# Gated linear attention and a two-layer MLP: block decay on TensorE and ScalarE, groups of two, a new order of work

## The chip, the cores and the metric

The kernel runs on one core of one Trainium2 chip. The metric is the device time of one execution in microseconds (us). Engines are named TensorE (PE in the profile, its weight loads PEld), the vector engine (DVE), ScalarE (ACT), GpSimd (POOL) and SyncE (SP, which only issues DMAs).

## What is computed

Two stages, the second fed by the first. The first is a gated recurrence over 768 steps for 4 x 8 heads of 48 values; the second is an MLP with a squared ReLU over the 3072 resulting rows of 384 values.

```python
def _attn_ref(q, k, v, alpha):
    state = np.zeros((B, H, D, D))
    for t in range(S):
        state = alpha[:, :, t, :, None] * state + np.einsum('bhd,bhe->bhde', k[:, :, t], v[:, :, t])
        y[:, :, t] = np.einsum('bhd,bhde->bhe', q[:, :, t], state)

def _moe_ref(x, w_in, w_out, s, b):
    h = x @ w_in
    r = np.maximum(h, 0.0)
    return (s * (r * r) + b) @ w_out
```

`w_in` is 384 x 2048, `w_out` 2048 x 384; all inputs and the output are float32, the matmuls run in bf16.

## The kernel before

**Tiling.** The 4 sequences of 768 steps are cut into 24 blocks of 128 steps, 6 to a sequence. Blocks 0 to 3 are done as two pairs (`pair_...`), blocks 4 to 23 one by one (`st_...`). For each block:

- `st_ln` (ScalarE) takes the logarithm of alpha; `st_cum` (TensorE) sums it over time with a triangular matrix, into `cum_ps`, a part of the PSUM bank `ct_ps`.
- `st_exp_b` and `st_exp_i` (ScalarE) give b, the running decay, and its inverse.
- `st_qb` (L433) and `st_kb` (L438), on the vector engine, scale q by b and k by the inverse. `st_vcast` (L427, GpSimd) casts v to bf16.
- `st_Tdma` (L455) transposes scaled q and k with one DMA transpose issued from ScalarE's queue. Blocks 0 to 3 are transposed on TensorE instead.
- `st_A` (L506) forms the scores q k^T, `st_mask` (L515, vector engine) masks them, and `st_y` (L544) forms the output from scores and v, and from q and the state of the block before.
- `st_KV` (L464) forms k^T v in a bank given by `p_of(n)` (`ct_ps` from block NKV on, `py_ps` before). `st_t1` (L485, L489) adds it to the state, and `st_snew` (L500, GpSimd) multiplies the sum by the decay of the whole block, the tile `blast`.
- `st_yevac` (ScalarE) copies the output from PSUM into `xd`, the input of the MLP.

**The block decay.** `blast` holds, for each head and key index, the decay over the block's 128 steps, laid out over partitions. Blocks 0 to 3 get it on TensorE: the logarithms are multiplied with a column of ones, and a small exponential follows. From block NBL = 4 on, `st_bl` gets it from the last row of b: a copy of 32 rows on GpSimd into `b_row` (L417), and two small DMAs from GpSimd's queue that spread the row over partitions (L422). The last block of a sequence needs none. All this is float32.

**The MLP.** The blocks are taken in groups of one or two (`GROUPS`). `mm1` (L709) multiplies weights with a group's `xd` into one of two banks, 512 columns at a time (4 slices of the hidden layer for a group of one, 2 for a group of two). `relu` (L718, ScalarE) and `square` (L724, vector engine) fill a ring of 12 blocks (`gt`), `mm2` (L771) multiplies by `w_out` in four quarters for each block, `oevac` (L782) scales and adds the bias, and `ostore` (L795) writes out: from SP, and for block STQ = 18 from GpSimd's queue. The weights arrive in eight parts, cast by the engines listed in `CE`.

**What sets the order.** There is no automatic scheduling. The class `Schedule` gets every step with its engine, an expected duration, a priority and the tiles it reads and writes; it lays the steps out in expected time, engine by engine, and emits them in that order. The priority is a due time: `want(n)`, from the block's place, `UNIT` and `LEAD`, plus an offset for each kind of step from the table `P`. Each engine runs its instructions in the emitted order and waits where a tile isn't ready. NAY is the block from which scores of block n and the output of block n - 1 are emitted together; NKV is named above. Until the first second-layer matmul, `fill` puts matmuls on zeros into TensorE's expected idle time.

Of the kernel before, what the change touches and what calls it, by code (L numbers as in the profile page):

```python
# [8 lines left out]
FP32 = mybir.dt.float32  # L9
BF16 = mybir.dt.bfloat16  # L10
# [4 lines left out]

VW = 144

GROUPS = [2, 2, 1, 1, 1, 1, 1, 1, 1, 1, 1, 2, 2, 2, 1, 2, 2]
UNIT = 0.295
LEAD = {1: 165.9, 2: 313.7, 4: 51.3}  # L20

NPE = 4

NAY = 10

RING = 12

# [4 lines left out]
TP = 1.45  # L32
LATE = 2.5
NY = 2
NKV = 10
NR2 = 2
STQ = 18
NBL = 4
TBL = 1.7
BLP = 49.5  # L40
TC2 = ["DVE", "DVE"]
VC2 = ["ACT", "ACT"]
CE = ["ACT", "DVE", "ACT", "ACT", "ACT", "ACT", "ACT", "ACT"]
TC = dict(ACT=1.4, DVE=0.87, POOL=2.0)
FILL_GAP = 0.2
COLD = 9.0

P_BM, P_CS, P_BMM = -5, -264.9, 436.0
P = dict(
    ln=60.4, cum=-21.17, eb=-43.71, ei=-25.37, vc=49.76, qb=-0.52, kb=0.09, T=60.15,  # L50
    Tc=-13.57, KV=3.78, t1=-20.78, sn=117.05, Ay=-30.04, A=-44.0, mk=-19.93, y=-36.45,
    ye=18.77, m1=-13.74, re=21.48, sq=1.75, m2=-13.14, oe=-42.62, vm=-2.86, ci=404.27,
    co=-1295.27, ls=140.41, vn=85.16,
)

LOADS = ["V0", "i0", "A0", "K0", "Q0", "A1", "V1", "Q1", "i1", "K1", "i2", "i3", "v4", "o0", "o1", "o2", "o3", "a4", "k4", "q4"]
# [1 line left out]
class Schedule:  # L58
# [8 lines left out]
    def op(self, eng, dur, prio, fn, *args, r=(), w=(), lat=0.08, lock=False):  # L67
        me = len(self.ops)
        deps = set()
        for x in r:  # L70
            if x in self.writer:
                deps.add(self.writer[x])
        for x in w:
            if x in self.writer:
                deps.add(self.writer[x])
            deps.update(self.readers.get(x, ()))
        for x in r:
            self.readers.setdefault(x, []).append(me)
        for x in w:
            self.writer[x] = me  # L80
            self.readers[x] = []
        self.ops.append((eng, dur, prio, fn, args, deps, lat, lock))
# [67 lines left out]
def kernel(  # L150
# [12 lines left out]
    nc = tc.nc  # L163
    ctx.enter_context(tc.manual_schedule())

    B, H, S, D = q.shape
    C = 128
    HC = C // 2
    NCH = S // C
    NP = H // 2  # L170
# [6 lines left out]
    sb = ctx.enter_context(tc.tile_pool(name="sb", bufs=1))  # L177
# [15 lines left out]
    def p_of(n):  # L193
        return (ct_ps if n >= NKV else py_ps)[:, 0:384].rearrange("a (p e) -> a p e", p=NP)

    def many(name, n, shape, dtype, zero=None):
        tiles = []
        for i in range(n):
            t = sb.tile(shape, dtype, name=f"{name}{i}")
            if zero is not None:  # L200
                zero.memset(t, 0.0)
            tiles.append(t)
        return tiles
# [63 lines left out]
    for j in range(2):  # L267
        part = mask2[HC * j : HC * j + HC].rearrange("a (j p) -> a j p", j=2)
        nc.gpsimd.affine_select(
            out=part,  # L270
            in_=part,
# [15 lines left out]
    b_sb = [b_all[:, i] for i in range(2)]  # L287
# [2 lines left out]
    qkT_all = sb.tile([128, 4, 2, NP, 128], BF16, name="qkT")  # L290
    qkT_sb = [qkT_all[:, i] for i in range(4)]
    am_sb = many("am", 2, [128, 2, NP, 128], BF16)
    blast_all = sb.tile([128, 4, NP], FP32, name="blast")
    nc.vector.memset(blast_all, 1.0)
    b_row = sb.tile([128, 2, 2, D, NP], FP32, name="b_row")
    blast_sb = [blast_all[:, i] for i in range(4)]
    xd_sb = many("xd", 3, [128, 3, 512], BF16)
    r_sb = many("r", 2, [128, 512], BF16)
# [91 lines left out]
    def st_cum(n):  # L390
        la = la_sb[n % 2]
        nc.tensor.matmul(  # L392
            out=cum_ps, lhsT=U_bf, rhs=la[:, :, 0:D], start=True, stop=True
        )
        if n % NCH == NCH - 1 or n >= NBL:
            return
        laf = la.rearrange("a h d -> a (h d)")
        for p in range(NP):
            nc.tensor.matmul(
                out=bl_ps[:, p : p + 1],  # L400
                lhsT=laf[:, 128 * p : 128 * p + 128],
                rhs=ones_col_bf,
                start=True,
                stop=True,
            )
# [3 lines left out]

    def st_exp_i(n):  # L410
        nc.scalar.activation(out=binv_sb[n % 2], in_=cum_ps, func=AF.Exp, scale=-1.0)  # L411
        if n % NCH != NCH - 1 and n < NBL:
            nc.scalar.activation(out=blast_sb[n % 4], in_=bl_ps, func=AF.Exp)

    def st_bl(n):
        rows = slice(C - 32, C)
        nc.gpsimd.tensor_copy(  # L417
            out=b_row[rows, n % 2].rearrange("a e d p -> a p e d"),
            in_=b_sb[n % 2][rows].rearrange("a (p e) d -> a p e d", e=2),
        )  # L420
        for e in range(2):
            nc.gpsimd.dma_start(  # L422
                out=blast_all[64 * e : 64 * e + D, n % 4, :], in_=b_row[C - 1 : C, n % 2, e]
            )

    def st_vcast(n):
        nc.gpsimd.tensor_copy(  # L427
# [251 lines left out]
    blk_group = []  # L679
    for g, m in enumerate(GROUPS):  # L680
        blk_group += [(g, t) for t in range(m)]
# [11 lines left out]
    quads = []  # L693
    for g, m in enumerate(GROUPS):
        per = 4 // m
        for u in range(NJ // per):
            units.append((g, [u * per + i for i in range(per)]))
        for tt in range(m):
            for jq in range(NJ // 4):
                quads.append((g, tt, jq))  # L700
    first_blk = [sum(GROUPS[:g]) for g in range(len(GROUPS))]

    def mm1(w):
        g, js = units[w]
        n = GROUPS[g] * C
        hp = h_ps[w % 2]
# [13 lines left out]
    def square(w):  # L720
        g, js = units[w]
        m, s0 = GROUPS[g], first_blk[g] % RING
        r = r_sb[w % 2].rearrange("a (i s t) -> a i s t", i=len(js), s=m)
# [75 lines left out]
    op = sched.op  # L799
    NG = len(GROUPS)  # L800

# [3 lines left out]
    def last(n):  # L805
        return n % NCH == NCH - 1

    def want(n):
        g, t = blk_group[n]
        return (4 * n - LEAD[GROUPS[g]]) * UNIT  # L810

# [21 lines left out]
    for rank, item in enumerate(loads):  # L833
        t, i = rank - 1000, int(item[1:])
# [15 lines left out]
        if st >= NST:  # L850
            reuse.append((len(sched.ops), [(x, h) for x in ("AQ", "KV")[st % 2]]))
        eng = CE[st]
        if item[0] == "i":
            op("SP", TW, t, load_w_in, i, st, w=key, lat=2.0)
            op(eng, TC[eng], P["ci"], cast_w_in, i, st, eng, r=key, w=[("wib", i)], lock=eng != "ACT")
        else:
# [3 lines left out]
               w=["colpart" if i else "colsum"], lock=True)  # L860
# [10 lines left out]
    def pb(n):  # L871
        return "ct" if n >= NKV else "py"

# [6 lines left out]
    def add_block(n):  # L880
        i2, i3, ii, s4 = n % 2, n % 3, n % NIN, n % 4
        t = want(n)
        qT = [("qkT", s4, 0), ("qkT", s4, 1)]
        vp = [("vp", s4, 0), ("vp", s4, 1)]
        if n < N1:
            if n % 2 == 0:
                add_pair(n // 2)
            c = n % 2
            op("PE", 0.5, t + P["KV"], pair_KV, n,
               r=[("kb", s4 - c), ("kb", s4 - c + 1), ("vp", s4, c), ("vc", n // 2 % 2, c)],  # L890
               w=[pb(n)], lat=0.16)
            finish_block(n)
            return
        if n >= N1 + NIN:
            for x in "aqkv":
                load_op(x, n)
        op("ACT", 0.45, t + P["ln"], st_ln, n, r=[("a", ii)], w=[("la", i2)])
        op("PE", 0.27 if n < NBL and not last(n) else 0.16, t + P["cum"], st_cum, n, r=[("la", i2)], w=["ct"], lat=0.16)
        op("ACT", 0.41, t + P["eb"], st_exp_b, n, r=["ct"], w=[("b", i2)])
        if n < NBL and not last(n):  # L900
            op("ACT", 0.49, t + P["ei"], st_exp_i, n, r=["ct"], w=[("bi", i2), ("bl", s4)])
        else:
            op("ACT", 0.41, t + P["ei"], st_exp_i, n, r=["ct"], w=[("bi", i2)])
            if not last(n):
                op("POOL", TBL, t + BLP, st_bl, n, r=[("b", i2)], w=[("bl", s4)], lat=3.4)
        op("POOL", 0.5, t + P["vc"], st_vcast, n, r=[("v", ii)], w=vp, lock=True)
        op("DVE", 0.48, t + P["qb"], st_qb, n, r=[("q", ii), ("b", i2)], w=[("qb", s4)], lock=True)
        op("DVE", 0.48, t + P["kb"], st_kb, n, r=[("k", ii), ("bi", i2)], w=[("kb", s4)], lock=True)
        if n < NPE:
            op("PE", 0.45, t + P["T"], st_T, n, r=[("qb", s4), ("kb", s4)], w=["ct"], lat=0.16)  # L910
            op("DVE", 0.61, t + P["Tc"], st_Tcopy, n, r=["ct"], w=qT)
        else:
            op("ACT", 1.25, t + P["T"], st_Tdma, n, r=[("qb", s4), ("kb", s4)],
               w=[("tq", s4)] + qT, lat=0.1)
            op("SP", 1.95, -3000, lambda: None, r=[("tq", s4)], w=qT, lat=2.0)
        if not last(n):
            op("PE", 0.17, t + P["KV"], st_KV, n, r=[("kb", s4)] + vp, w=[pb(n)], lat=0.16)
        finish_block(n)
# [40 lines left out]
    def finish_block(n):  # L959
# [9 lines left out]
        rA, wA = qT, ["a"]  # L969
        late = n + 1 < NBLK and n + 1 >= NAY  # L970
        if n >= NAY:
            r1, w1 = ys.pop(n - 1)
# [12 lines left out]
    def add_group(g):  # L985
# [7 lines left out]
        for u in range(NJ // per):  # L993
            w = unit_i
            unit_i += 1
            js = units[w][1]
            t = w * UNIT
            op("PE", {1: 0.67, 2: 0.656, 4: 0.648}[m], t + P["m1"], mm1, w,
# [5 lines left out]
        for u in range(4 * m):  # L1004
# [5 lines left out]
            ob = (x // 4) % 2  # L1010
            t = (x + 4 * m + P["m2"]) * UNIT
            op("PE", 0.65, t, mm2, x,
# [18 lines left out]
    for n in range(NBLK):  # L1031
        add_block(n)

        if n and n >= NAY and blk_group[n - 1][0] != blk_group[n][0]:
            add_group(blk_group[n - 1][0])
        if (n + 1 < NAY or n + 1 == NBLK) and n + 1 == first_blk[blk_group[n][0]] + GROUPS[blk_group[n][0]]:
            add_group(blk_group[n][0])
# [46 lines left out]
```

## Time and profile before

| what | value |
|---|---|
| median of 3 runs | 190.92 us (190.63 to 192.15) |
| the profiled execution | 190.63 us, of which its span 188.9 us |
| granted TensorE clock, mean | 0.991 |
| bytes moved by DMA | 35.51 MB, mean 188 GB/s |
| ScalarE: relu (L718), 96 of them | 55.7 us |
| vector engine: square (L724), 96 / mask (L515), 24 | 42.5 / 29.3 us |
| DMA transposes, issue to landing | 2.7 to 7.7 us, median 4.6 |

How to read it: all times are from one execution, counted from the start of its span. A row names a line of the kernel, the engine, the operation, the tile written and those read. Busy time is given with the mean duration of one instruction; behind the bar stands how long the engine sat idle just before such instructions, and what ended most of that. The 40-digit rows cut the span into 40 slices of 4.7 us; a 9 is a share of 90% or more. Matmuls overlap, so a matmul's duration (some 0.22 us for 128 columns) is longer than the distance from one start to the next, and distances between starts tell what TensorE can do. The profile follows the chain of waits only from 94.24 us on.

### The profile page before, as it was taken

Reading aid. Unit: us, or ns where it says so; the run is one execution under the profiler, and the core shown is the slowest. Engines: PE = TensorE matmul, PEld = TensorE weight load, DVE = VectorE, ACT = ScalarE, POOL = GpSimd, SP = SyncE. Lnnn points to the kernel's source line nnn. Section 1 sums busy time; section 2 is a strip of 40 time slices with the busy share of each in tenths; the row PEclk is TensorE's granted clock in tenths of the full one; section 3 lists DMA queues with packets and bytes.
Section 4 is the critical chain, followed back from the end, with each engine's and each line's share of the span. In section 5 each row is a group of like instructions: output and inputs, shape, how many; then the busy total and the mean of one; then the engine's idle time right before and its main releaser. Section 6 shows DMA issues by size and latency. Waiting matters only on the chain. (4 is left out here: it accounts for less than half of the span.)

```text
span 188.9 us, 5578 instructions
## 1 busy us (share of the span) xinstructions
PE 172.8 (91%) x2232; PEld 124.0 (66%) x2232; DVE 139.6 (74%) x252; ACT 106.3 (56%) x200; POOL 71.1 (38%) x118
## 2 busy tenths in 40 slices
PE   6669987899999997999999999999969999999992
PEld 2245765566776875877776767777647786778672
DVE  2468999998688788967877797979756987464421
ACT  3466899943553863655564555856515753566400
POOL 7973022255506356323645553334436532010000
PEclk9999999999999999999999999999979999999999
DMA  5999998999999999998998999999697693011012
GB/s 157 358 341 372 347 372 220 210 159 247 219 183 211 243 125 229 181 219 183 211 208 169 182 188 230 187 210 210 131 164 168 112 213 96 9 42 45 33 51 83
DMA packets 120985, 35.51 MB, mean 188 GB/s; under 512 B 114256, under 2 KB 119376, under 8 KB 120960
## 3 DMA queue, kind: packets, MB, share of 16 engines
q1 hardware_dynamic: 98688, 29.70, 67.5%
q10 hardware_dynamic: 21120, 5.25, 20.0%
q0 software_dynamic: 1152, 0.22, 0.7%
q8 instruction: 17, 0.28, 0.6%
q14 instruction: 8, 0.07, 0.1%
HBM read 25.17 MB, written 4.72 MB: 158 GB/s over the span
## 5 line engine op out<-in xcount | busy, mean ns | idle before, releaser
L718 ACT ACTIVATE r<-h_ps 128x512 bf16<-128x512 f32 x96 | 55.7, 599 | 38.1 <-PE h_ps L709 14.9
L709 PE MATMUL h_ps<-xd,w_in_bf 128*128 128x128 bf16 (+1 forms) x816 | 74.6, 243 | 0.7 <-ACT r L718 0.7
L771 PE MATMUL o_ps<-w_out_bf,gt 128*128 128x384 bf16 x368 | 71.0, 328 | 1.4 <-ACT w_out_bf L324 1.3
L709 PEld LDWEIGHTS <-w_in_bf 128*128 128x128 bf16 x816 | 61.3, 98 | 11.8 <-issue 2.2
L724 DVE TENSOR_TENSOR gt<-r 128x512 bf16<-128x512 bf16 x96 | 42.5, 457 | 15.3 <-ACT r L718 14.5
L771 PEld LDWEIGHTS <-gt 128*128 128x128 bf16 x368 | 34.3, 98 | 19.5 <-issue 1.9
L417 POOL COPY b_row<-b_s 32x384 f32<-32x384 f32 x16 | 17.2, 1077 | 42.4 <-ACT b_s L408 40.0
L515 DVE TENSOR_TENSOR am<-a_ps,mask 128x1024 bf16<-128x1024 f32 x24 | 29.3, 1220 | 3.7 <-PE a_ps L506 3.5
L500 POOL TENSOR_TENSOR s_st<-s_st,blast 128x384 bf16<-128x384 bf16 x16 | 14.2, 887 | 23.5 <-DMA blast<-b_row 10.1
L782 DVE SCALAR_TENSOR_TENSOR o_sb<-o_ps,s_col,bias_w 128x384 f32<-128x384 f32 x23 | 14.1, 615 | 8.2 <-PE o_ps L771 7.9
L422 POOL DMA_DIRECT2D blast<-b_row x32 | 16.7, 526 | 4.7 <-POOL b_row L417 4.7
L689 ACT ACTIVATE xd<-py_ps 128x384 bf16<-128x384 f32 x22 | 11.1, 503 | 10.9 <-PE py_ps L544 3.4
L438 DVE TENSOR_TENSOR qk<-k_in,binv 128x384 bf16<-128x384 f32 x20 | 15.8, 792 | 0.0
L427 POOL CAST vp<-v_in 128x384 bf16<-128x384 f32 x20 | 10.5, 527 | 13.9 <-PE a_ps L506 7.0
L386 ACT ACTIVATE la<-a_in 128x384 bf16<-128x384 f32 x20 | 10.5, 525 | 8.1 <-DVE am L515 2.7
L433 DVE TENSOR_TENSOR qk<-q_in,b_s 128x384 bf16<-128x384 f32 x20 | 12.8, 639 | 2.6 <-ACT b_s L408 2.4
L408 ACT ACTIVATE b_s<-ct_ps 128x384 f32<-128x384 f32 x20 | 9.8, 492 | 4.9 <-DVE gt L724 2.6
L506 PE MATMUL a_ps<-qkT 64*128 64x128 bf16 x192 | 9.6, 218 | 1.7 <-DMA qkT<-qk 1.3
L506 PEld LDWEIGHTS <-qkT 64*128 64x128 bf16 x192 | 5.5, 94 | 7.9 <-issue 4.7
L411 ACT ACTIVATE binv<-ct_ps 128x384 f32<-128x384 f32 x20 | 9.9, 493 | 0.0
L489 DVE TENSOR_TENSOR s_st<-ct_ps,s_st 64x192 bf16<-64x192 f32 x18 | 6.4, 354 | 4.0 <-PE ct_ps L464 2.0
L544 PE MATMUL py_ps<-am,vp 128*32 128x128 bf16 x352 | 8.8, 219 | 0.0
(92 smaller groups left out, 128.9 us busy)
## 6 DMA issues: line engine op xcount, KB each, us to landing
out_dram<-o_sb SPq DMA_DIRECT2D x22, 192.0 KB, 2.7
v_in<-in_v_dram SPq DMA_DIRECT2D x20, 192.0 KB, 4.5
a_in<-in_alpha_dram SPq DMA_DIRECT2D x20, 192.0 KB, 4.3
k_in<-in_k_dram SPq DMA_DIRECT2D x20, 192.0 KB, 4.1
q_in<-in_q_dram SPq DMA_DIRECT2D x20, 192.0 KB, 4.6
wst<-in_moe_w_in_dram SPq DMA_DIRECT2D x4, 768.0 KB, 6.8
gt<-in_moe_w_out_dram SPq DMA_DIRECT2D x4, 768.0 KB, 9.6
gt<-in_alpha_dram SPq DMA_DIRECT2D x2, 384.0 KB, 4.5
```

Source lines behind the costliest of these rows:

```text
L417: nc.gpsimd.tensor_copy(out=b_row[rows, n % 2].rearrange("a e d p -> a p e d"), in_=b_sb[n % 2][rows].rearrange("a (p e) d -> a p e d", e=2),)
L422: nc.gpsimd.dma_start(out=blast_all[64 * e : 64 * e + D, n % 4, :], in_=b_row[C - 1 : C, n % 2, e])
L433: nc.vector.tensor_tensor(out=qk_sb[n % 4][:, 0, :, 0:D], in0=q_in[n % NIN], in1=b_sb[n % 2], op=ALU.mult)
L438: nc.vector.tensor_tensor(out=qk_sb[n % 4][:, 1, :, 0:D], in0=k_in[n % NIN], in1=binv_sb[n % 2], op=ALU.mult,)
L500: nc.gpsimd.tensor_tensor(out=s_sb[n % 3], in0=t1_sb[n % 2], in1=bl, op=ALU.mult)
L506: nc.tensor.matmul(out=a_ps[:, e, p, :], lhsT=qkT[64 * e : 64 * e + 64, 1, p, :], rhs=qkT[64 * e : 64 * e + 64, 0, p, :], start=True, stop ...
L515: nc.vector.tensor_tensor(out=am_sb[n % 2].rearrange("a e p t -> a (e p) t"), in0=a_ps.rearrange("a e p t -> a (e p) t"), in1=(mask2 if n ...
L709: nc.tensor.matmul(out=hp[:, i * n : (i + 1) * n], lhsT=w_in_bf[:, kk, 128 * j : 128 * (j + 1)], rhs=xd_sb[g % 3][:, kk, 0:n], start=(kk = ...
L718: nc.scalar.activation(out=r_sb[w % 2], in_=h_ps[w % 2], func=AF.Relu)
L724: nc.vector.tensor_tensor(out=gt_sb[:, s0 : s0 + m, js[0] : js[0] + len(js)].rearrange("a s j t -> a j s t"), in0=r, in1=r, op=ALU.mult,)
L771: nc.tensor.matmul(out=op[:, 0:d_model], lhsT=gt_sb[:, s0, j], rhs=w_out_bf[:, j, :], start=(j == 0), stop=(j == NJ - 1),)
L782: nc.vector.scalar_tensor_tensor(out=ots, in0=o_ps[(x // 4) % 2][:, 0:d_model], scalar=s_col, in1=bias_w, op0=ALU.mult, op1=ALU.add,)
```

## The change

The block decay of blocks 4 to 22 is formed as in blocks 0 to 3: four one-column matmuls on TensorE behind the cumulative sum, and a small exponential on ScalarE behind `st_exp_i`. `st_bl`, `b_row` and its DMAs go, `blast` becomes bf16, and the clearing of `blast` goes. Four blocks form groups of one, where there were ten. The first part of `w_in` is cast by GpSimd instead of ScalarE. k^T v moves to the bank `ct_ps` from block 7 on (block 10 before), scores and output are paired from block 12 (10 before), and all due times are others. Transposes and the output store from GpSimd are the same in both.

```diff
-GROUPS = [2, 2, 1, 1, 1, 1, 1, 1, 1, 1, 1, 2, 2, 2, 1, 2, 2]
-UNIT = 0.295
-LEAD = {1: 165.9, 2: 313.7, 4: 51.3}
+GROUPS = [2, 2, 1, 1, 1, 1, 2, 2, 2, 2, 2, 2, 2, 2]
+UNIT = 0.392
+LEAD = {1: 204.6, 2: 323.1, 4: 100.0}
...
-NAY = 10
+NAY = 12
...
-NKV = 10
+NKV = 7
...
-NBL = 4
-TBL = 1.7
-BLP = 49.5
...
-CE = ["ACT", "DVE", "ACT", "ACT", "ACT", "ACT", "ACT", "ACT"]
+CE = ["POOL", "DVE", "ACT", "ACT", "ACT", "ACT", "ACT", "ACT"]
...
-P_BM, P_CS, P_BMM = -5, -264.9, 436.0
+P_BM, P_CS, P_BMM = -5, -286.4, 473.5
 P = dict(
-    ln=60.4, cum=-21.17, eb=-43.71, ei=-25.37, vc=49.76, qb=-0.52, kb=0.09, T=60.15,
+    ln=34.88, cum=-15.29, eb=-32.24, ei=9.49, vc=73.43, qb=-9.65, kb=14.71, T=95.62,
...
-    blast_all = sb.tile([128, 4, NP], FP32, name="blast")
-    nc.vector.memset(blast_all, 1.0)
-    b_row = sb.tile([128, 2, 2, D, NP], FP32, name="b_row")
+    blast_all = sb.tile([128, 4, NP], BF16, name="blast")
...
-        if n % NCH == NCH - 1 or n >= NBL:
+        if n % NCH == NCH - 1:
             return
         laf = la.rearrange("a h d -> a (h d)")
         for p in range(NP):
...
         nc.scalar.activation(out=binv_sb[n % 2], in_=cum_ps, func=AF.Exp, scale=-1.0)
-        if n % NCH != NCH - 1 and n < NBL:
+        if n % NCH != NCH - 1:
             nc.scalar.activation(out=blast_sb[n % 4], in_=bl_ps, func=AF.Exp)
-
-    def st_bl(n):
-        rows = slice(C - 32, C)
-        nc.gpsimd.tensor_copy(
-            out=b_row[rows, n % 2].rearrange("a e d p -> a p e d"),
-            in_=b_sb[n % 2][rows].rearrange("a (p e) d -> a p e d", e=2),
-        )
-        for e in range(2):
-            nc.gpsimd.dma_start(
-                out=blast_all[64 * e : 64 * e + D, n % 4, :], in_=b_row[C - 1 : C, n % 2, e]
-            )
...
-        if n < NBL and not last(n):
-            op("ACT", 0.49, t + P["ei"], st_exp_i, n, r=["ct"], w=[("bi", i2), ("bl", s4)])
-        else:
-            op("ACT", 0.41, t + P["ei"], st_exp_i, n, r=["ct"], w=[("bi", i2)])
-            if not last(n):
-                op("POOL", TBL, t + BLP, st_bl, n, r=[("b", i2)], w=[("bl", s4)], lat=3.4)
+        op("ACT", 0.49, t + P["ei"], st_exp_i, n, r=["ct"], w=[("bi", i2), ("bl", s4)])
```

The rest of the table `P` is replaced in the same way, and the planner's time for the cumulative sum is that with the four matmuls for all blocks.

More of the change, by code (lines that the diff above doesn't have):

```diff
@@ L46 @@
 COLD = 9.0
-P_BM, P_CS, P_BMM = -5, -264.9, 436.0
+P_BM, P_CS, P_BMM = -5, -286.4, 473.5
 P = dict(
-    ln=60.4, cum=-21.17, eb=-43.71, ei=-25.37, vc=49.76, qb=-0.52, kb=0.09, T=60.15,
-    Tc=-13.57, KV=3.78, t1=-20.78, sn=117.05, Ay=-30.04, A=-44.0, mk=-19.93, y=-36.45,
-    ye=18.77, m1=-13.74, re=21.48, sq=1.75, m2=-13.14, oe=-42.62, vm=-2.86, ci=404.27,
-    co=-1295.27, ls=140.41, vn=85.16,
+    ln=34.88, cum=-15.29, eb=-32.24, ei=9.49, vc=73.43, qb=-9.65, kb=14.71, T=95.62,
+    Tc=-13.62, KV=-13.54, t1=9.55, sn=124.73, Ay=-11.39, A=-22.53, mk=-58.68, y=-13.83,
+    ye=5.65, m1=-19.67, re=9.86, sq=-33.02, m2=-18.25, oe=-24.3, vm=-57.17, ci=324.52,
+    co=-825.8, ls=148.33, vn=-450.01,
 )
@@ L897, in add_block @@
         op("ACT", 0.45, t + P["ln"], st_ln, n, r=[("a", ii)], w=[("la", i2)])
-        op("PE", 0.27 if n < NBL and not last(n) else 0.16, t + P["cum"], st_cum, n, r=[("la", i2)], w=["ct"], lat=0.16)
+        op("PE", 0.27, t + P["cum"], st_cum, n, r=[("la", i2)], w=["ct"], lat=0.16)
         op("ACT", 0.41, t + P["eb"], st_exp_b, n, r=["ct"], w=[("b", i2)])
-        if n < NBL and not last(n):
-            op("ACT", 0.49, t + P["ei"], st_exp_i, n, r=["ct"], w=[("bi", i2), ("bl", s4)])
-        else:
-            op("ACT", 0.41, t + P["ei"], st_exp_i, n, r=["ct"], w=[("bi", i2)])
-            if not last(n):
-                op("POOL", TBL, t + BLP, st_bl, n, r=[("b", i2)], w=[("bl", s4)], lat=3.4)
+        op("ACT", 0.49, t + P["ei"], st_exp_i, n, r=["ct"], w=[("bi", i2), ("bl", s4)])
         op("POOL", 0.5, t + P["vc"], st_vcast, n, r=[("v", ii)], w=vp, lock=True)
```

## The prediction

> **What bounds the kernel now.** I read the page's shares and 40 slices first, then the waits by total, then TensorE's own timeline at the places where it stands still.
>
> ```profile
> PE 172.8 (91%) x2232; PEld 124.0 (66%) x2232; DVE 139.6 (74%) x252; ACT 106.3 (56%) x200; POOL 71.1 (38%) x118
> PE   6669987899999997999999999999969999999992
> PEclk9999999999999999999999999999979999999999
> DMA  5999998999999999998998999999697693011012
> L417 POOL COPY b_row<-b_s 32x384 f32<-32x384 f32 x16 | 17.2, 1077 | 42.4 <-ACT b_s L408 40.0
> L422 POOL DMA_DIRECT2D blast<-b_row x32 | 16.7, 526 | 4.7 <-POOL b_row L417 4.7
> ```
>
> TensorE's row is full from slice 10 to the end save for one dip, in which its clock row falls to 7: after the first 40 us TensorE sets the time, and what can be won is its standing still there. GpSimd is 38% busy, and 33.9 us of its 71.1 are the two decay rows (L417, L422). TensorE's timeline shows the dip:
>
> ```profile
> 136.68 0.41 PE L544 MATMUL py_ps<-am,vp 128*32 128x128 bf16 x16
> 138.83 0.46 PE L464 MATMUL ct_ps<-vp,qk 128*128 128x96 bf16 x4 [1.75 <-POOL vp L427]
> 139.09 1.48 PE L771 MATMUL o_ps<-w_out_bf,gt 128*128 128x384 bf16 x4
> 140.37 2.42 PE L709 MATMUL h_ps<-xd,w_in_bf 128*128 128x256 bf16 x12
> ```
>
> The k^T v product waits 1.75 us for GpSimd's cast of v. The next four second-layer matmuls then take 1.28 us to the next start, against 0.65 us elsewhere, and twelve first-layer ones 2.26 us against 1.31. The chain of waits shows what GpSimd did:
>
> ```profile
> 134.26 0.55 DVE qk L438
> ...
> 134.91 0.93 POOL s_st L500
> 135.84 0.05 issue
> 135.89 1.00 POOL b_row L417
> 136.89 0.28 issue
> 137.17 1.06 POOL blast L422 x2
> 138.23 0.05 issue
> 138.28 0.51 POOL vp L427
> ```
>
> k's scaled tile was ready at 134.81; the cast came 3.5 us later, behind one state product, one copy and two DMA issues. Vector engine rows show a second cost: at 97.17 the same k product (L438) took 1.08 us and at 134.26, with no GpSimd copy beside it, 0.55.
>
> [...]eight of the 20 L438 rows and three of the L433 rows begin while an L417 copy runs and take 0.82 to 1.09 us instead of 0.55, some 5 us in all.[...] eight 2-column matmuls of L585 start at 6.05 and the next matmul at 6.25, 25 ns each.[...] 1.75 us of idleness were followed by 3.5 us at about half rate[...].
>
> **The change, part by part.** The sum is made against the profiled execution, 190.63 us (span 188.9 and 1.73 around it); the median of the runs is 190.92, 0.3 above.
>
> *Decay back on TensorE.* Sixteen blocks (4 to 22 without the last of each sequence) get four one-column matmuls: 64 x 25 ns = **+1.6 us**, on the path since TensorE has no room. ScalarE gets 16 small exponentials; the nearest row (L602, eight columns) lasts 183 ns, so at most 2.9 us, beside a ScalarE that is 56% busy. They stand after both large exponentials, so q's and k's products don't wait for them; a relu behind one does, by up to 0.18 us. I take 0 here and put that into new waits.
>
> *Decay off GpSimd.* 16 copies and 32 DMA issues go. Four stalls of TensorE go with them: 1.75 (above), 0.17 at 94.28 (also for the cast), 0.25 at 98.31 (for the k product stretched to 1.08 us), and 0.37 at 101.01 (the cumulative sum waits for the state sum, L489, which waits for the state product at 99.37, behind a copy and two issues): **-2.5 us**. The half-rate stretch costs 0.63 + 0.95 + 0.09 = 1.7 us. It begins with the stall, so I take **-1.7**; a 1.34 us wait at 72 us has none after it, so its bounds are 0 and -1.7. The small DMAs are 0.7% of DMA time: 0. The decay as bf16 changes no row that TensorE waits for now: 0.
>
> *Groups.* Six blocks go from groups of one to groups of two. A one-block group's 24 narrow matmuls take 1.35 us per half (48.74 to 50.09), so 2.68 a block; twelve wide ones take 1.31 us, 2.62 a block. 6 x 0.06 = **-0.4 us**. TensorE issues one filler matmul fewer, some **-0.2** before the first second-layer matmul.
>
> *First weight cast on GpSimd.* ScalarE did it in 1.47 us at 11.66. GpSimd's cast row is 527 ns for 384 columns; four times that is an estimate of 2.1 us, from 11.5 to 13.6. Behind it on GpSimd's queue are the second pair's four casts of v (from 12.54 to 13.6) and the state product at 15.51, which slips by some 0.5 us. Their readers are the shift on TensorE at 15.40 and the output of block 2 after 25: hidden. The first reader of the weights starts at 17.84. ScalarE's logarithm of pair 1 moves up, but the sums behind it hold their place on TensorE after block 1's output, so no gain. I take 0, bounds -0.5 and +0.5[...].
>
> *New order.* I counted TensorE's work between producer and consumer in both instruction orders with the rates above. From a block's cumulative sum to its score product (the way through both exponentials, the products and the DMA transpose) the 20 blocks have 7.6 to 11.6 us now, eight of them at most 8.5; in the new order 7.8 to 13.3, four at most 8.5. The one stall there now (1.34 us at 73.39, for a transpose) belongs to block 8, which goes from 8.0 to 9.0: I take half, **-0.7**, bounds 0 and -1.3. Other distances shrink. From cumulative sum to k^T v, three blocks (12, 16, 20) fall to 2.9 us and four (8, 9, 13, 21) to 3.4 to 3.6; the work takes 1.8 us when nothing is in the way (133.00 to 134.81) and 2.0 to 3.3 in other places. From scores to output, blocks 4, 7, 8 and 9 have 1.9 to 2.2; the trace needs 1.9 (44.60 to 46.49). From k^T v to the next sum, blocks 8 and 9 have 1.2, since k^T v now moves to the shared bank (ct_ps) at block 7 instead of 10; the trace needs 1.2 when the vector engine is free (106.06 to 107.24). Nine or so of these at 0.2 us each: **+1.8**, bounds 0 and +6, for nothing in the trace before shows them. The store of block 18 stays on GpSimd, last in its queue, now with no decay ahead: 0. On SP the stores stand a few places earlier or later among the loads; SP's loads mostly wait for buffers, and the load that came last ahead of a cast (3.4 us late at 156.27) stopped only GpSimd. At the end 52 instead of 36 second-layer matmuls follow the last first-layer one: same work, no gap now, 0.
>
> *Sum:* +1.6 - 2.5 - 1.7 - 0.4 - 0.2 - 0.7 + 1.8 = -2.1. From 190.63 that is 188.5; from the median 188.8. I say **188.6 us**, 1.2% faster. The case's own range, with the clock stretch kept or no new waits, is 187.0 to 190.0.
>
> **Rivals.** (a) *The gain is eaten by the order.* New waits come to 3.5 to 4.5 us, or loads and transposes, with the DMA row at 9 in nearly every slice to 150 us, push back when TensorE runs ahead. For it: the distances above, and landing times of the transpose from 2.7 to 7.7 us. Against: some 0.5 us a block goes from the way to the transpose, and fewer blocks are near the limit. Time: 188.5 + 2.2 = 190.7. (b) *A stall of the shared bank, slower.* At blocks 8 and 9 the cumulative sum waits for the state sum. If that stands behind a score mask (1.22 us) on the vector engine, the sum, both exponentials and the transpose come 1.2 us later, and scores in turn. Two places where that grows to the size of the stall at 138.83, each followed by a half-rate stretch, cost 2 x (1.75 + 1.7) = 6.9 us in place of the 1.8: 193.6. It decides once new waits pass 6.1 us (192.8). Against: vector load falls by the 5 us of stretched products. (c) *The decay was no burden.* GpSimd's stalls come back at the cast for another reason (a late load of v, 6.3 us of waits in three places now); only +1.6 - 0.6 and the new waits count: 191.6 without these, 193.4 with 1.8 of them. The instruction order shows the copies and issues gone, so the change does do what it says.
>
> **How the numbers follow.** Forecast 0.50, (a) 0.20, (b) 0.18, (c) 0.12. About 1%, 1.9 us, is what can be told from no change, so faster means under 189.0. Of the forecast 0.40 lies below that and 0.10 above; a little of (a) lies below: faster 0.43. Same: 0.10 + 0.16 + 0.06 = 0.32. Slower: (b), half of (c) and an edge of (a): 0.25. The range, 186.9 to 193.4, leaves out a tenth on each side: below, no new waits with the startup bound; above, most of (b).
>
> **What would show it.** Right: no L417 or L422 rows; GpSimd near 39 us busy; L438 near 0.55 us mean (0.79 now) outside state products; TensorE's waits on the cast under 0.3 us; no clock below 9 after 20 us; 64 one-column matmuls adding 1.6 us. Wrong: TensorE waiting over 4 us after 40 us for DVE (s_st, am, qk) or qkT, a first second-layer matmul later than 28.5 us, or a new half-rate stretch.

## The result and the profile after

| | before | after |
|---|---|---|
| median of 4 runs each, same chip | 190.85 us (190.63 to 192.15) | 185.22 us (184.53 to 185.95) |
| ratio, 95% interval | | 0.9692 (0.9634 to 0.9749) |
| profiled execution, span | 190.63, 188.9 us | 185.07, 183.4 us |
| granted TensorE clock, mean | 0.991 | 1.000 |

The changed kernel is 5.6 us faster; 2.1 to 2.3 were forecast, and the time lies below the range. Measured again beside other experiments it had a ratio of 0.9812 (0.9764 to 0.986) and 186.63 us, so "some 2 to 3%" is what can be said of its gain; the two intervals do not overlap. The direction was right; the size was too small, by a factor of 2.5 in the first pair and of about 1.7 in the second.

The page after, the shares and slices that answer to those of before, and two rows of its groups:

```profile
PE 171.9 (94%) x2151; PEld 122.8 (67%) x2151; DVE 135.4 (74%) x251; ACT 106.0 (58%) x215; POOL 39.6 (22%) x71
PE   6678987999999999999989999999999999999993
PEclk9999999999999999999999999999999999999999
DMA  5999999999999999899999999999965992000112
L411 POOL CAST vp<-v_in 128x384 bf16<-128x384 f32 x20 | 11.9, 593 | 63.8 <-DMA v_in<-in_v_dram 63.8
L422 DVE TENSOR_TENSOR qk<-k_in,binv 128x384 bf16<-128x384 f32 x20 | 11.6, 582 | 1.1 <-DMA k_in<-in_k_dram 1.0
```

The dip of TensorE's row and of its clock is gone, GpSimd is busy 39.6 us instead of 71.1, and no row of a copy or a DMA issue of the decay is left. k's product (L422 now, L438 before) has fallen from a mean of 792 ns to 582. DMA is as full as before (194 GB/s in the mean, 188 before), so the gain does not come from there.

The table splits each span at the start of the first second-layer matmul (`mm2`) and at the end of the last matmul, and gives the sum of TensorE's waits after 40 us.

| part, us | before | after | difference |
|---|---|---|---|
| up to the first second-layer matmul | 28.15 | 27.22 | -0.93 |
| from there to the last matmul's end | 157.21 | 153.05 | -4.16 |
| after it | 3.56 | 3.09 | -0.47 |
| within the middle: TensorE's waits after 40 us | 4.60 (7 places) | 1.81 (5 places) | -2.79 |
| within the middle: half-rate stretch | 1.7 | none | -1.7 |
| within the middle: wait for the column sums | 0.89 | 0.26 | -0.63 |

With +1.6 for the one-column matmuls, -0.4 for wider groups and +0.2 for a wait on the second weights' cast, the last three rows make -3.7 of the -4.2. TensorE's waits before, by what it waited for, those that matter here (total us, times, longest):

```profile
PE ct_ps L464 <- POOL vp L427: 1.9, 2, 1.8
...
PE a_ps L506 <- DMA qkT<-qk: 1.3, 1, 1.3
...
PE o_ps L373 <- DVE colsum L356: 0.9, 1, 0.9
PE h_ps L709 <- ACT r L718: 0.7, 2, 0.4
```

and after:

```profile
PE h_ps L693 <- ACT r L702: 0.8, 2, 0.5
...
PE py_ps L528 <- DVE am L499: 0.3, 1, 0.3
PE o_ps L755 <- DVE gt L708: 0.3, 1, 0.3
PE ct_ps L448 <- POOL vp L411: 0.3, 1, 0.3
PE o_ps L368 <- DVE colsum L351: 0.3, 1, 0.3
```

Nothing that TensorE waits for after 40 us in this trace is late by more than 0.5 us. The wait for the cast has shrunk to 0.30 us in one place, and the transpose isn't waited for at all. (In a second trace of the changed kernel three waits are left, of 0.72, 0.54 and 1.07 us: a relu, a transpose and that same cast. Ahead of the cast GpSimd stands idle in both traces, for v's load.) The third line of before is one that the prediction passed over. Its cause stands in the timeline of before, all engines, at the place where the column sums for the bias are folded:

```profile
36.53 1.11 POOL L417 COPY b_row<-b_s 32x384 f32<-32x384 f32 x1 [6.38 <-ACT b_s L408]
36.82 1.06 DVE L356 TENSOR_TENSOR colsum<-colsum 128x384 f32<-128x384 f32 x1
```

The fold starts while a GpSimd copy of the decay runs and takes 1.06 us, and TensorE waits for it. After, the groups with different shapes kept apart show:

```profile
L351 DVE TENSOR_TENSOR colsum<-colsum 128x384 f32<-128x384 f32 x1 | 0.6, 551 | 0.0
...
L394 PE MATMUL ct_ps<-ones_col_bf,la 128*128 128x1 bf16 x64 | 3.9, 164 | 0.0
```

Half the time, without the copy. The second row is the price of the change: the 64 one-column matmuls. Its "busy" 3.9 us is not their cost, since matmuls overlap; four of them take 0.10 us from the first's start to the next matmul's (60.54 to 60.64), 1.6 us in all.

### The profile page after: what moved, and what is told of

It is laid out like the page before. It is cut to its first block, busy times and chain, and to the rows that moved or that the text cites. A ratio compares the mean times of both kernels' runs of the same rounds, so it can differ in the third digit from the quotient of the medians.

```text
span 183.4 us, 5347 instructions
## 1 busy us (share of the span) xinstructions
PE 171.9 (94%) x2151; PEld 122.8 (67%) x2151; DVE 135.4 (74%) x251; ACT 106.0 (58%) x215; POOL 39.6 (22%) x71
## 4 chain that ended last, share of the span: by engine, by line
PE 44%; DVE 3%; DMA 2%; issue 1%; ACT 1%; ACTq 1%; SPq 0%; POOL 0%; POOLq 0%
PE o_ps L755 19%; PE h_ps L693 17%; PE py_ps L528 3%; DMA v_in<-in_v_dram 2%; PE a_ps L490 2%; PE o_ps L724 1%; PE ct_ps L448 1%; DVE gt L708 1%; PE ct_ps L387 1%; ACT r L702 1%; DVE o_sb L766 1%; ACTq L439 1%; DVE qk L422 1%; DVE am L499 0%; PE h_ps L724 0%
## 5 line engine op out<-in xcount | busy, mean ns | idle before, releaser
L693 PE MATMUL h_ps<-xd,w_in_bf 128*128 128x256 bf16 (+1 forms) x672 | 73.2, 257 | 0.9 <-ACT r L702 0.8
L702 ACT ACTIVATE r<-h_ps 128x512 bf16<-128x512 f32 x96 | 55.1, 600 | 28.4 <-PE h_ps L693 9.4
L755 PE MATMUL o_ps<-w_out_bf,gt 128*128 128x384 bf16 x368 | 69.1, 326 | 1.9 <-ACT w_out_bf L319 1.5
L693 PEld LDWEIGHTS <-w_in_bf 128*128 128x128 bf16 x672 | 56.2, 98 | 10.7 <-issue 1.5
L411 POOL CAST vp<-v_in 128x384 bf16<-128x384 f32 x20 | 11.9, 593 | 63.8 <-DMA v_in<-in_v_dram 63.8
L473 DVE TENSOR_TENSOR s_st<-ct_ps,s_st 64x192 bf16<-64x192 f32 x24 | 8.5, 354 | 6.1 <-PE ct_ps L448 5.3
L422 DVE TENSOR_TENSOR qk<-k_in,binv 128x384 bf16<-128x384 f32 x20 | 11.6, 582 | 1.1 <-DMA k_in<-in_k_dram 1.0
L1028 PE MATMUL o_ps<-zeros 128*128 128x512 bf16 x21 | 7.0, 463 | 1.3 <-DVE zeros L236 1.3
L528 PEld LDWEIGHTS <-vp 128*32 128x32 bf16 x384 | 6.5, 97 | 1.2 <-issue 0.7
```

Of the source, the lines that this page charges most:

```text
L411: nc.gpsimd.tensor_copy(out=vp_sb[n % 4].rearrange("a p (x d) -> a p x d", d=D)[:, :, 0:3:2, :], in_=v_in[n % NIN].rearrange("a (p e) d -> ...
L422: nc.vector.tensor_tensor(out=qk_sb[n % 4][:, 1, :, 0:D], in0=k_in[n % NIN], in1=binv_sb[n % 2], op=ALU.mult,)
L528: nc.tensor.matmul(out=y_of(n)[32 * (x % 4) : 32 * (x % 4) + 32, x // 4, :], lhsT=(st[:, p, c0 : c0 + 32] if e is None else vp[:, p, c0 + ...
L693: nc.tensor.matmul(out=hp[:, i * n : (i + 1) * n], lhsT=w_in_bf[:, kk, 128 * j : 128 * (j + 1)], rhs=xd_sb[g % 3][:, kk, 0:n], start=(kk = ...
L702: nc.scalar.activation(out=r_sb[w % 2], in_=h_ps[w % 2], func=AF.Relu)
L755: nc.tensor.matmul(out=op[:, 0:d_model], lhsT=gt_sb[:, s0, j], rhs=w_out_bf[:, j, :], start=(j == 0), stop=(j == NJ - 1),)
```

## The experiments

The question was which part brings the gain: the decay off GpSimd, or the new order with its groups and cast; and within the decay, which of its costs. The kernels of the first four share a chip and a before of 190.21 us (15 runs), the next four one of 190.01 us (12 runs), the last four one of 191.06 us (11 runs).

**1. The decay alone, every engine in the old order.** In the kernel before:

```diff
-        if n % NCH == NCH - 1 or n >= NBL:
+        if n % NCH == NCH - 1:
             return
...
-        if n % NCH != NCH - 1 and n < NBL:
+        if n % NCH != NCH - 1:
...
-                op("POOL", TBL, t + BLP, st_bl, n, r=[("b", i2)], w=[("bl", s4)], lat=3.4)
+                op("POOL", TBL, t + BLP, lambda n: None, n, r=[("b", i2)], w=[("bl", s4)], lat=3.4)
```

> The order of before on every engine, only the decay of blocks 4 to 22 moved from GpSimd and its DMAs to TensorE and ScalarE. Decay theory (GpSimd's copies and DMA issues made TensorE wait, at the cast of v, the state and the stretched vector products): the 1.6 us of one-column matmuls is paid, stalls of 1.75 + 0.17 + 0.25 + 0.37, the half-rate stretch of 1.7, the 1.34 us wait for block 8's transpose and 0.5 us at the fold of column sums go: about 186.5 to 187.5 us. Order theory (the gain is in the new order and the groups of two, the decay itself is neutral): 190.9 + 1.6, 191.5 to 192.5 us.

Measured: 185.7 us, ratio 0.9741 (0.966 to 0.9821). TensorE's waits after 40 us come to 1.29 us in four places, none of them one of the seven of before. The longest, in its timeline:

```profile
140.95 0.40 PE L506 MATMUL a_ps<-qkT 64*128 64x128 bf16 x8 [0.51 <-DMA qkT<-qk]
```

That is a late block. The scores that waited 1.34 us for their transpose at 73.39 before start at 72.83 without a wait. (They are the tenth scores in TensorE's timeline and belong to the sixth of the 20 transposes, so to block 9; the prediction and the expectation call it block 8.) So the decay alone is about the whole gain, and rival (c), that the decay was no burden, falls.

**2. The new order alone, the decay left on GpSimd.** In the changed kernel, `st_bl` as it was before, called directly behind `st_exp_i`'s first exponential for blocks 4 to 22:

```diff
-        if n % NCH == NCH - 1:
+        if n % NCH == NCH - 1 or n >= 4:
             return
...
-        if n % NCH != NCH - 1:
-            nc.scalar.activation(out=blast_sb[n % 4], in_=bl_ps, func=AF.Exp)
+        if n % NCH != NCH - 1 and n >= 4:
+            st_bl(n)
```

> The changed kernel with its new order on every engine, but the decay of blocks 4 to 22 formed by GpSimd's copy and two DMAs, put on GpSimd's queue where the small exponential stood. Decay theory: 1.6 us of matmuls go and 4 to 6 us of stalls come back, 187.5 to 189.5 us. Order theory: 183.6 to 185.5 us.

Measured: 201.82 us, ratio 1.059 (1.0505 to 1.0675). TensorE waited 8.2 us in six places for the cast of v and 3.6 in two for the state sum. What GpSimd did ahead of one such wait, in its timeline:

```profile
59.82 1.06 POOL L419 DMA_DIRECT2D blast<-b_row  x2 [0.29 <-POOL b_row L414]
...
64.81 0.86 POOL L497 TENSOR_TENSOR s_st<-s_st,blast 128x384 bf16<-128x384 bf16 x1 [3.39 <-DMA blast<-b_row]
65.73 0.95 POOL L414 COPY b_row<-b_s 32x384 f32<-32x384 f32 x1
66.98 1.05 POOL L419 DMA_DIRECT2D blast<-b_row  x2 [0.29 <-POOL b_row L414]
68.08 0.50 POOL L424 CAST vp<-v_in 128x384 bf16<-128x384 f32 x1
```

The state product stands 3.39 us for the small DMAs' data (18.1 us in seven places over the kernel), and the cast behind it comes when product, copy and two issues are through. This is the cost of the decay at this place in this order; another place for it, tuned to the order, wasn't tried. Two stretches at half rate after 20 us add to it in this trace (experiment 7). It shows that the order is not a gain by itself, and how much hangs on what is queued ahead of the cast.

**3. The bias product later, in the kernel before.** At 13.48 us, in the startup, TensorE stood 1.47 us for the first state sum on the vector engine. That sum stood behind the product that fills `bones` with the bias, which waited 1.28 us for a small DMA. So the product was moved behind block 1's mask:

```diff
+        if n == 1:
+            bias_mul()
...
-    op("DVE", 0.3, P_BM, bias_mul, r=["b"], w=["bones"], lock=True)
+    op("DVE", 0.3, P_BM, lambda: None, r=["b"], w=["bones"], lock=True)
```

> Before, with one vector instruction (the product of ones with the bias column, which waits for a small DMA) moved from ahead of the first state product to behind the second score mask, where the changed kernel has it. Startup theory (the vector engine's 1.28 us wait there delayed TensorE's first products, and all that follows, by 1 us): 189.7 to 190.1 us. Rival (the delay is absorbed before the first second-layer matmul, which waits for the casts of its weights): 190.7 to 191.0 us.

Measured over 12 runs: 189.83 us, ratio 0.9984 (0.9944 to 1.0025). The wait itself shrank from 1.47 to 0.39 us, and the time didn't move by what can be measured: the first second-layer matmul started at 28.74 us, no earlier than the 28.15 of before. With the old decay still in, the old stalls are there again at nearly the same times, as TensorE's timeline shows:

```profile
72.68 0.40 PE L506 MATMUL a_ps<-qkT 64*128 64x128 bf16 x8 [0.61 <-DMA qkT<-qk]
...
138.51 0.33 PE L464 MATMUL ct_ps<-vp,qk 128*128 128x96 bf16 x4 [1.40 <-POOL vp L427]
```

Block 9's transpose is late by 0.61 us here and the cast at 138 by 1.40; before it was 1.34 and 1.75. They belong to the old decay, not to one execution.

**4. Experiments 1 and 3 together.**

> Both edits in the order of before. If both theories hold and add up: 185.5 to 186.5 us, so that order, groups and the cast on GpSimd are left with less than 1.3 us of the gain. If the new order is needed for more than that: above 187 us.

Measured: 185.18 us, ratio 0.9735 (0.9656 to 0.9813); again beside the changed kernel 186.44 us, 0.9794 (0.974 to 0.9847):

> The order of before with the decay on TensorE and the late bias product, again. From the first second-layer matmul to the last matmul its trace had 151.8 us, the changed kernel's 153.1. If that holds for the time: 0.3 to 0.8% faster than the changed kernel on this chip. If the first 28 us, which differ from run to run, decide: no difference.

The changed kernel once more, on that chip:

> The changed kernel once more, on the same chip and beside the same runs of before as the next two, to put a figure on what the new order, the groups and the cast add to the decay. If they add nothing: within 0.5% of the next run. If they are worth the 1.1 us between the ratios so far: 0.5 to 0.8% below it. Expected ratio to before 0.965 to 0.975.

It gave 186.63 us, 0.9812 (0.9764 to 0.986). On one chip the changed kernel and the old order with the new decay differ by 0.1%, within both intervals. So new order, groups and first cast together add nothing that can be measured. The middle part, from the first second-layer matmul to the last matmul, is 153.1 us in both traces of the changed kernel, 153.3 in experiment 1, 151.8 and 152.1 here.

**5. The parts of the old decay, one by one.** All in the changed kernel, with `blast` still formed by TensorE, so that nobody waits for their results. Only the 16 copies:

```diff
+            if n >= 4:
+                st_bl(n)
+
+    def st_bl(n):
+        rows = slice(C - 32, C)
+        nc.gpsimd.tensor_copy(
+            out=b_row[rows, n % 2].rearrange("a e d p -> a p e d"),
+            in_=b_sb[n % 2][rows].rearrange("a (p e) d -> a p e d", e=2),
+        )
```

> The changed kernel with GpSimd's 16 copies of b's last rows added back, read by nobody: no DMAs, the decay still from TensorE. [...]at least half of the way back from e2, 189 us or more, with the k product near 0.8 us mean. Queue theory (what hurt is GpSimd's time ahead of the cast of v, and the wait of the state product for the small DMAs): 1.1 us a block hides in a GpSimd that is 22% busy; 185 to 187 us.

Measured over nine runs: 188.73 us, ratio 0.9906 (0.9853 to 0.996). "189 us or more" stood for the case that the loss comes from the vector engine's products taking longer beside the copies (k's 792 ns on average before, 582 after). The groups with shapes apart:

```profile
L352 DVE TENSOR_TENSOR colsum<-colsum 128x384 f32<-128x384 f32 x1 | 1.1, 1055 | 0.0
...
L432 DVE TENSOR_TENSOR qk<-k_in,binv 128x384 bf16<-128x384 f32 x20 | 15.7, 785 | 0.5 <-DMA k_in<-in_k_dram 0.5
```

The copies alone bring back both stretched rows, k's product at 785 ns (792 before the change) and the fold at 1055. The fold goes with these copies in all 14 traces: 1.05 to 1.06 us in the five with them (before, experiments 2, 3, this one and copies with issues), 0.55 us in the nine without. TensorE's wait for it is 0.87 to 0.89 us in the five and 0.38 or less in eight of the nine; in the ninth (experiment 6, first kernel) it is 1.16, for a fold that started late and took 0.55.

Only the 32 issues, of a constant row into a tile that nobody reads:

```diff
+    def st_bl(n):
+        for e in range(2):
+            nc.gpsimd.dma_start(
+                out=scr[64 * e : 64 * e + D, n % 4, :], in_=b_row[C - 1 : C, n % 2, e]
+            )
```

> The changed kernel with only the 32 small DMA issues on GpSimd's queue added back, from a constant tile to a tile that nobody reads. They wait for nothing and no engine waits for them. Queue theory in its weaker form (the issuing time of 1.06 us a block is the cost): 187 us or more. If the cost is in waiting for the data: 185 to 186 us.

Measured: 186.69 us, ratio 0.9826 (0.9769 to 0.9884), a little above the changed kernel's 0.9692 and 0.9812 and inside the interval of the second: at most a small cost, and none that these runs can show.

Copies and issues, the issues into the same unread tile:

> Both added back, copies and issues in the places of the run with the decay on GpSimd, but nothing waits for their data, since the decay comes from TensorE. Against that run (201.8 us) it lacks only the wait of the state product and of the first state for the small DMAs, and has the 1.6 us of matmuls. If waiting for the data made most of the loss: under 192 us. If GpSimd's own time made it: 198 us or more.

Measured: 191.69 us, ratio 1.0103 (1.0034 to 1.0172). TensorE waits 5.5 us in seven places for the cast. The parts don't simply add: against the two ratios of the changed kernel, copies alone cost 0.9 to 2.1 points, issues alone 0.1 to 1.3, both together 2.9 to 4.1. The waits suggest why: TensorE waits for the cast once with copies alone (1.23 us) and once with issues alone (1.13), at the one cast that is late in the changed kernel too, and seven times with both. That fits a cast that is late only when what stands ahead of it is longer than its slack. From here to experiment 2 are 10.1 us more (201.82), and what that one adds is the state product's wait for the DMAs' data, against 1.6 us of one-column matmuls that it doesn't have. In its profiled run the two half-rate stretches after 20 us account for some 3 us, an estimate from the spacing of starts in them. The two befores, 190.21 and 190.01, differ by 0.1%.

**6. More casts to GpSimd.** The second part of `w_out` in the changed kernel, to relieve ScalarE (`eng = "POOL" if i == 1 else eng` in `cast_w_out`):

> A try for a faster version: the changed kernel in its order, with the second part of the output weights cast by GpSimd, idle at that time, instead of ScalarE. TensorE waits 0.96 us for that cast now, and ScalarE is free 1.4 us sooner. If the casts set the pace there: 183.7 to 184.7 us. If the column sums on the vector engine set it (TensorE then waits for them before the bias product)[...]: 185 to 186 us.

Measured: 187.7 us, ratio 0.9866 (0.9806 to 0.9926), not faster. TensorE waits 0.8 us for that cast and 1.2 for the fold of the column sums, where the changed kernel's two traces have 0.85 to 0.96 and 0.26 to 0.37: the wait moved.

The first part of `w_in`, as in the change, but in the kernel of experiment 4 with its order kept:

```diff
+        eng = "POOL" if i == 0 else eng
```

> The same order, with the first part of w_in cast by GpSimd instead of ScalarE, the step for which the prediction took 0 with bounds of 0.5 us. Hidden: within 0.5 us of the run without it. If GpSimd's later casts of v for the second pair hold TensorE up: 0.5 to 1 us slower. If ScalarE was late there: 0.5 us faster.

Measured: 184.80 us (184.29 to 185.72), ratio 0.9721 (0.9664 to 0.9777). All six runs lie below all six of the changed kernel on the same chip (186.33 to 186.99), 1.0% in the medians, so this is the fastest version here; the two intervals against before overlap, and so do the ranges of this kernel and of the one without the cast (185.15 to 187.01). It has one stall of TensorE after 40 us, 0.29 us. In the changed kernel's trace this cast took 1.46 us (at 11.58), not the 2.1 that I estimated. Against the same kernel without it, the medians differ by 1.6 us on this chip, but on the chip of the first four that kernel had nearly the same ratio (0.9735). So whether the cast brings anything there is not settled. In the traces TensorE's wait for a weight cast at 20 us went from 0.90 to 0.50 us (for another producer) and one of 0.69 at 52 us is absent, which would be a part of it.

**7. Does a long gap bring the half rate?** The kernel of experiment 4, with three useless GpSimd copies ahead of five casts, to make gaps of different lengths:

```diff
+        if n in (9, 13, 15, 19, 21):
+            for _ in range(3):
+                nc.gpsimd.tensor_copy(out=scr, in_=qk_sb[n % 4])
```

> The same kernel as the second, with three useless copies on GpSimd, which wait for the scaled k of the block, ahead of the cast of v in blocks 9, 13, 15, 19 and 21, so that TensorE waits for that cast as it did at 138.83 before. If every wait of 1.5 us or more starts a half-rate stretch of some 3.4 us: each gap is followed by first-layer matmuls at twice their spacing and costs 1.7 us more than itself. If it is chance: some gaps of 1.5 to 2.8 us are followed by full rate.

One run, 193.28 us, with waits on the cast of up to 1.91 us. TensorE's timeline after the longest:

```profile
97.50 0.33 PE L468 MATMUL ct_ps<-vp,qk 128*128 128x96 bf16 x4 [1.91 <-POOL vp L431]
97.67 1.46 PE L777 MATMUL o_ps<-w_out_bf,gt 128*128 128x384 bf16 x8
98.97 0.33 PE L393 MATMUL ct_ps<-la,U_bf 128*128 128x384 bf16 x1
```

Eight second-layer matmuls take 1.30 us to the next start, full rate. In the trace of experiment 2, TensorE at three gaps:

```profile
68.63 0.33 PE L461 MATMUL ct_ps<-vp,qk 128*128 128x96 bf16 x4 [2.33 <-POOL vp L424]
...
70.08 2.74 PE L706 MATMUL h_ps<-xd,w_in_bf 128*128 128x128 bf16 x24
...
95.39 0.32 PE L389 MATMUL ct_ps<-la,U_bf 128*128 128x384 bf16 x1 [2.66 <-DVE s_st L482]
95.55 3.41 PE L768 MATMUL o_ps<-w_out_bf,gt 128*128 128x384 bf16 x20
...
120.97 0.48 PE L461 MATMUL ct_ps<-vp,qk 128*128 128x96 bf16 x4 [2.79 <-POOL vp L424]
...
122.79 1.46 PE L706 MATMUL h_ps<-xd,w_in_bf 128*128 128x256 bf16 x6
124.05 0.38 PE L389 MATMUL ct_ps<-la,U_bf 128*128 128x384 bf16 x1
```

After 2.33 us of gap the 24 narrow matmuls take 2.74 us instead of 1.50, the half rate; after 2.66 us twenty second-layer ones take 3.41, 0.17 each, full rate. After 2.79 us six first-layer ones take 1.26 us to the next start instead of 0.66, half rate again. Gap length alone doesn't decide it.

The granted clock shows the same stretches. In the trace of before it is 0.50 from 138.89 to 142.30 us, for 3.41 us, and 1.00 on both sides. In experiment 2 its mean over windows of 5 us is 0.95 and 0.71 from 65 and 70 us, 0.66 from 120 us, and 1.00 in the windows next to these; if it was 0.50 there too, that is some 3.4 us in each of the two places, an estimate from these means. What decides, beside the length of a gap, was not shown. The trace with the made gaps has no clock record.

## Why the prediction was right and wrong

**What bounds the kernel: right.** TensorE's standing still in the middle is where the time was, and the middle part gave 4.2 of the span's 5.6 us. **Cost of the new matmuls and of the groups: right**, +1.6 and -0.4 by the spacing of starts (two narrow halves of 1.35 us are 2.70 and not 2.68, which makes it nearer -0.5). **GpSimd to near 39 us busy (39.6), k's product near 0.55 (0.58), the clock at 9 throughout: as listed.** (Three other profiles, one of them the changed kernel's second, ran slower from some 11 to 18 us: eight k^T v products of that second one, from 12.78 us, start 0.08 us apart, those of the first trace from 12.43 us 0.04, and in experiment 2 and with the copies alone the mean clock of the first 30 us is 0.89, where the first trace has 1.00.) The wait for the cast, listed as under 0.3 us, was 0.30 and, in the second trace, 1.07.

**"Four stalls go, -2.5", and "half of block 8's transpose wait, -0.7": the step that failed.** All 4.60 us of stalls of the old trace went, 1.4 more than these two terms. I had listed the stalls that a copy or an issue explains and left two waits for the relu (0.42 and 0.30) and half of the transpose wait standing, and then added +1.8 for the waits of the new order. But waits of an order belong to it as a whole. When it is replaced, all of the old ones are taken out and all of the new ones put in; the sum kept a part of the old and counted the new in full. Nor did it need the new order: in experiment 1, with the old order kept, all seven waits of before are gone and 1.29 us of others have come. So the old waits hung on the decay more widely than through the four stalls that the prediction could trace to a copy or an issue.

The transpose is the clearest case. It belongs to block 9, not to block 8, so the distance of 8.0 going to 9.0 was read for the wrong block: between block 9's cumulative sum and its scores the traces have, waits left out, 8.7 us before and 9.0 after. Its wait of 1.34 us is gone with the old order kept, and experiment 3, old order and old decay, has it at 0.61. The longer distance in the new order wasn't needed. What became shorter is the DMA itself: from issue to landing this transpose took 7.7 us before and 7.0 in experiment 3, and 4.4 to 5.3 in the five traces of the old order with the new decay. Why this one did is open, since the mean over all transposes of a trace is 4.6 to 5.0 us with and without the old decay.

**"New waits, +1.8": 1.81 in the profile, by size.** The five places are two relu waits (0.35 and 0.50), one mask (0.35), one second-layer input (0.31) and one k^T v (0.30), where I had nine places at cumulative sums, scores, outputs and k^T v. Only the mask and the k^T v are of the listed kinds; the total agrees by luck, and the same kernel's second trace has 2.33 in three places.

**The fold of the column sums, not in the sum.** I read that eleven of the k and q products began beside a GpSimd copy and took 0.82 to 1.09 us instead of 0.55, and priced this only where those products were waited for. The same copy stood beside the fold at 36.53, and TensorE waited 0.63 us longer for it. The fold takes 551 ns without the copies and 1055 with them alone, though the copy covers 32 partitions and the fold 128.

**"Half-rate stretch, -1.7": right in the trace, not assured.** It went with the stall. But experiment 3, the kernel before with one step moved, has a gap of 1.40 us at the same place and no half rate, and the made gaps have one of 1.91. So the term was worth less than 1.7 on average. Without it the forecast would have been -0.4 us. Yet the 17 of the 38 runs of before beside the experiments with a mean granted clock of 0.998 or more have a median of 189.5 us, and the six runs of the changed kernel at that clock one of 185.7: nearly 4 us without half rate, though not all on one chip.

**Startup at -0.2 and tail at 0: -0.93 and -0.47 in this pair of traces.** The first second-layer matmul started anywhere from 27.2 to 29.6 us over all 14 traces, and at 27.22 and 28.79 in two of the changed kernel. So the -0.93 isn't the change's, and "later than 28.5 us" was no sign of anything: the changed kernel's second trace passes it and is still about 2% faster. The tail was 3.5 us or a little more in both traces of the old order with the old decay, 3.4 in one other and 3.1 in the remaining eleven; why is open. The step "first weight cast, 0" can't be read out of the changed kernel. In the old order the medians put it at 1.6 us, beyond the bound of 0.5, but this is not assured (experiment 6).

Against the forecast of -2.1: 1.4 for stalls kept by mistake, 0.63 for the fold, and 0.73 (0.93 without the forecast 0.2) and 0.47 at the ends make 3.2 of the 3.5 missing in the profiled pair. **The rivals:** (a) wanted 3.5 to 4.5 us of new waits, 1.81 and 2.33 came; (b) wanted stalls at blocks 8 and 9, none came; (c) fell with experiment 1, though the late load of v that it named does stand behind the one cast that is still late. The forecast's mechanism was right, and the range was too narrow below: its lower end took in the startup bound, but none of the remaining old stalls.

What stays open: whether this order has any worth of its own. It isn't better than the old one with the same decay in these runs, and worse by 5.9% than before with the old decay at the place tried.

## What to carry to other kernels

When a change replaces the order of work, take all waits of the old order out of the sum, not those with a known culprit alone, and put all of the new one in. A helper that is busy only 38% of the time can still hold the bottleneck: count what is queued ahead of the instruction that the bottleneck waits for, and every row of another engine that runs beside it, one-off steps included (here a fold of 0.55 us took 1.06 beside a copy). Let two traces of an unchanged part tell how much it varies before a difference there is explained.

## What the runs showed of the hardware

- Half rate of TensorE followed gaps of 1.75 us (before), 2.33 and 2.79 us (experiment 2), but not of 1.40 us at the same place (experiment 3), 1.91 us (made gaps) or 2.66 us (experiment 2). The granted clock was 0.50 for 3.41 us in the trace of before. What makes a gap bring it is not settled.
- The fold of the column sums, a 128x384 float32 operation of the vector engine with two inputs, took 1.05 to 1.06 us in the five traces with the GpSimd copies of 32 partitions, and 0.55 us without them.
- In the changed kernel GpSimd cast 128x1536 from float32 to bf16 in 1.46 us; ScalarE took 1.47 before. GpSimd's 128x384 casts there took 0.50 to 0.84 us, 0.51 in the median: four small ones would be 2.0 us, an estimate from that median.
